# A transformer block on one core: the moving operand of every float32r matmul read as two interleaved halves

## The chip, the cores and the metric

The kernel runs on one core of a Trainium2 chip. A core has a matrix engine (TensorE, called PE in the profile, with its weight loads as PEld), VectorE (DVE), ScalarE (ACT), GpSimd (POOL), and SyncE (SP), which issues the DMAs here. The metric is the device time of one launch in microseconds. Three runs of the kernel before gave 734.32, 734.81 and 735.09 us; their median is 734.81.

## The reference

The input x has 2048 tokens of 448 elements. The program is one pre-norm transformer block: causal attention in a sliding window of 256 tokens with 16 heads of 28 elements, then a GEGLU feed-forward with 1792 hidden columns.

```python
def _A_ref(x, wqkv, wo):          # H = 16, Dh = 28, W = 256
    qkv = ...(x @ wqkv)...
    scores = jnp.einsum("bhqd,bhkd->bhqk", q, k) * (Dh ** -0.5)
    mask = (idx[:, None] - idx[None, :] >= 0) & (idx[:, None] - idx[None, :] < W)
    scores = jnp.where(mask[None, None], scores, -1e9)
    o = jnp.einsum("bhqk,bhkd->bhqd", _softmax(scores, axis=-1), v)
    return (...o...) @ wo

def _B_ref(x, w_gate, w_up, w_down):
    h = _gelu(x @ w_gate) * (x @ w_up)
    return h @ w_down

h = x + _A_ref(_layernorm(x), A_wqkv, A_wo)
h2 = h + _B_ref(_layernorm(h), B_w_gate, B_w_up, B_w_down)
```

Everything is float32.

## The kernel before

**Numbers.** Most products run as float32r matmuls, a float32 format that TensorE takes in one pass. To keep the accuracy of float32, an operand is split into a high part (a copy rounded to float32r, `to_hi`, line 327, on ACT) and a low part (the remainder, `to_lo`, line 330, on DVE or POOL). A product is then a sum of terms: high times high, high times low, low times high. For a contraction over 448 rows, `TERMS` lists 11 matmuls that accumulate into one PSUM bank.

**Attention.** Four groups of four heads by four chunks of 512 tokens make 16 blocks. For each, `project_tile` (line 569) computes queries and keys transposed, with 512 tokens as moving columns (line 580); ACT and DVE take the bank as high and low part (lines 584 and 585), and DMAs carry both through DRAM into the tiles rq and rk. `values` (line 530) computes v with 224 moving columns (line 535) and ACT copies it out (line 538). `scores` (line 621) computes scores of up to 384 keys (line 629), and DVE adds the mask and takes the row maximum (line 633). `maxima` carries the negated maxima into extra rows of rq, so that `probs` (line 693) gives shifted, transposed scores (line 701), from which ACT's exponential writes the tile pp (line 705). `attend` multiplies pp with v in plain float32, four 29-column matmuls side by side (line 735), `drain` divides by the row sums, and `output` (line 770) applies wo with six matmuls of 448 columns (line 779); DVE adds the result to the residual hres (line 782).

**Feed-forward.** The 14 slices of 128 hidden columns are taken in groups of 3, 4, 4 and 3; for each group the kernel goes through the four chunks of 512 tokens, which makes 56 products. The first four (n = 0 to 3) use full 128-row matmuls (line 927) for gate and up. From n = 4 on, a product issues pairs of 64-row matmuls (`pair`, line 899, matmul on line 903): one works in the upper and one in the lower half of the array, on different banks. Phase 0 has 10 pairs of 512 columns and phase 1 has 11, with the halves exchanged; the down product of an earlier hidden slice adds 12 pairs of 448 columns, six between the phases and six after them. Where halves change banks, `seen` (line 909) lets ACT read one word of the bank, so that the next matmul into it waits for the first phase. ACT applies GELU straight from the bank (line 965), DVE multiplies with the other bank (line 967), ACT and DVE split the result (lines 969 and 970). The last down product has 12 full matmuls (line 992), and DVE adds each finished bank to hres (line 998).

**Order.** The instructions are not issued where they stand. Each is registered with `op(engine, cost, latency, key, function, reads, writes, bank)`, and `Lists.run` simulates the six queues with these costs, picks the next instruction of each engine by key among those that can start, and assigns PSUM banks. `mm(n)` is the planner's cost of a matmul of n columns. Engines then run their own queues in order and wait on semaphores. In the feed-forward the order of the matmuls is fixed by a chain of dependences at the end of `feed_forward`.

## Time and profile before

The profiled execution took 734.23 us, of which the span from the first to the last instruction is 732.5 us.

| what | value |
|---|---|
| median of three runs | 734.81 us |
| profiled execution | 734.23 us, span 732.5 us |
| PE busy | 723.8 us, 99% |
| PE weight loads busy | 604.6 us, 83% |
| DVE, ACT, POOL busy | 395.9, 365.8, 160.3 us |
| mean granted TensorE clock | 0.999 |
| HBM read, written | 48.23 MB, 29.36 MB |

The page gives each engine's busy time and share of the span, then the chain of work that ended last, followed back from the last instruction. Rows of groups give line, engine, operation, output and input tiles, shapes and count, then the busy time and the mean ns of one, then the idle time before the group and what ended it. Rows of the timeline give the start, the time from that start to the end of the last of a merged run, and the count. A matmul's recorded time includes its way through the array, so consecutive matmuls overlap in the record, and the distance between starts tells what one costs.

### The profile page before, as it was taken

What the parts mean: (1) busy time and instruction counts of PE and PEld (TensorE: products, weight loads), DVE (VectorE), ACT (ScalarE), POOL (GpSimd) and SP (SyncE); (2) the same over time, 40 slices, a digit from 0 to 9 for tenths busy, and PEclk for the clock granted to TensorE, in tenths of its full rate; (3) what the DMA queues carried; (4) which work ended last, traced back from release to release, by engine and by line L of the source; (5) the groups of instructions that cost most, each with busy time, mean ns of one, the idle gap of its engine ahead of it and who ended that gap; (6) DMA issues with size and microseconds to landing.
All of it is one profiled execution on the core that took longest, in us unless ns stands there. A gap on an engine that the chain in (4) does not pass through costs nothing.

```text
span 732.5 us, 15381 instructions
## 1 busy us (share of the span) xinstructions
PE 723.8 (99%) x5893; PEld 604.6 (83%) x5893; DVE 395.9 (54%) x1057; ACT 365.8 (50%) x930; POOL 160.3 (22%) x253
## 2 busy tenths in 40 slices
PE   8999999999999999999999999999999999999997
PEld 7887888788888787768888888888888888888886
DVE  7977876776677788748554223144223243233223
ACT  7668776667666888876553222243222233222221
POOL 5615343343344547462000000000000000000000
PEclk9999999999999999999999999999999999999999
DMA  8888445755565777514652000012100000001012
GB/s 285 260 280 248 146 148 179 202 178 156 162 201 160 191 229 206 147 36 102 153 174 88 1 2 1 1 43 84 43 1 2 1 1 2 1 1 52 11 42 101
DMA packets 83138, 79.12 MB, mean 108 GB/s; under 512 B 34104, under 2 KB 72952, under 8 KB 83064
## 3 DMA queue, kind: packets, MB, share of 16 engines
q1 hardware_dynamic: 83064, 78.14, 35.3%
q8 instruction: 46, 0.75, 0.4%
q14 instruction: 28, 0.23, 0.1%
HBM read 48.23 MB, written 29.36 MB: 106 GB/s over the span
## 4 chain that ended last, share of the span: by engine, by line
PE 93%; ACT 2%; DVE 2%; DMA 1%; issue 1%; POOL 0%; SPq 0%; DVEq 0%; ACTq 0%; POOLq 0%
PE bank L903 52%; PE bank L580 9%; PE bank L701 6%; PE bank L629 6%; PE bank L735 6%; PE bank L535 5%; PE bank L779 5%; PE bank L927 2%; PE bank L383 1%; ACT pp L705 1%; DVE mt L633 1%; ACT xT L328 0%; DVE hres L782 0%; DMA hres<-in_x_dram 0%; PE bank L660 0%
## 5 line engine op out<-in xcount | busy, mean ns | idle before, releaser
L633 DVE CUSTOM_DVE_ANT_0 mt<-bank,mt 128x384 bf16<-128x384 f32 (+2 forms) x256 | 127.5, 524 | 38.2 <-PE bank L629 36.4
L705 ACT ACTIVATE pp<-bank 128x384 f32<-128x384 f32 (+2 forms) x352 | 121.5, 388 | 52.4 <-PE bank L701 46.5
L967 DVE TENSOR_TENSOR mt<-bank,mt 128x512 f32<-128x512 f32 x54 | 37.1, 688 | 139.5 <-ACT mt L965 139.5
L716 POOL TENSOR_SCALAR_AFFINE_SELECT pp<-pp 128x512 f32<-128x512 f32 x120 | 75.5, 642 | 124.8 <-ACT pp L705 115.0
L580 PE MATMUL bank<-xT,proj 128*128 128x512 f32 x308 | 101.2, 402 | 0.0
L701 PE MATMUL bank<-rq,rk 104*128 104x384 f32 (+2 forms) x352 | 96.8, 305 | 0.9 <-ACT pp L705 0.6
L965 ACT ACTIVATE mt<-bank 128x512 f32<-128x512 f32 x54 | 32.2, 596 | 113.5 <-PE bank L903 113.5
L629 PE MATMUL bank<-rk,rq 84*128 84x384 f32 (+2 forms) x256 | 82.7, 344 | 0.1
L903 PE MATMUL bank<-xT,rec 64*128 64x512 f32 x656 | 82.0, 388 | 0.0
L903 PE MATMUL bank<-xT,rk 64*128 64x512 f32 x656 | 82.0, 388 | 0.0
L701 PEld LDWEIGHTS bank<-rq,rk 104*128 104x128 f32 x352 | 64.7, 189 | 19.3 <-ACT pp L705 4.8
L903 PEld LDWEIGHTS bank<-xT,rec 64*128 64x128 f32 x656 | 63.0, 184 | 12.2
L903 PEld LDWEIGHTS bank<-xT,rk 64*128 64x128 f32 x656 | 63.0, 184 | 12.2
L998 DVE TENSOR_TENSOR hres<-bank,hres 128x448 f32<-128x448 f32 x64 | 35.5, 616 | 66.1 <-PE bank L903 63.9
L328 ACT ACTIVATE proj<-mt 128x512 fp32r<-128x512 f32 x54 | 34.1, 631 | 71.8 <-DVE mt L967 52.5
L903 PE MATMUL bank<-xT,proj 64*128 64x512 f32 x533 | 66.7, 388 | 0.0
L909 ACT ACTIVATE word<-bank 1x1 f32<-1x1 f32 x162 | 25.6, 158 | 79.2 <-PE bank L903 78.6
L580 PEld LDWEIGHTS bank<-xT,proj 128*128 128x128 f32 x308 | 55.9, 190 | 6.0 <-issue 0.8
L535 PE MATMUL bank<-proj,xT 128*128 128x224 f32 x352 | 60.2, 278 | 0.1
L903 PEld LDWEIGHTS bank<-xT,proj 64*128 64x128 f32 x533 | 51.1, 184 | 10.1 <-ACT word L909 0.3
L331 DVE TENSOR_TENSOR proj<-mt,proj 128x512 fp32r<-128x512 f32 x54 | 37.3, 691 | 36.8 <-ACT proj L328 28.5
L535 PEld LDWEIGHTS bank<-proj,xT 128*128 128x128 f32 x352 | 53.0, 191 | 1.8 <-DVE hres L782 0.3
(117 smaller groups left out, 1106.6 us busy)
## 6 DMA issues: line engine op xcount, KB each, us to landing
rk<-k SPq DMA_DIRECT2D x44, 336.0 KB
rq<-q SPq DMA_DIRECT2D x32, 336.0 KB
q<-proj SPq DMA_DIRECT2D x15, 448.0 KB
raw<-in_ffn_dram SPq DMA_DIRECT2D x7, 736.0 KB
v<-in_ffn_dram SPq DMA_DIRECT2D x7, 736.0 KB
k<-proj SPq DMA_DIRECT2D x11, 448.0 KB
hres<-in_x_dram SPq DMA_DIRECT2D x16, 224.0 KB
out_dram<-hres SPq DMA_DIRECT2D x16, 224.0 KB
```

The lines of the kernel that those rows point to most:

```text
L331: (eng or nc.vector).tensor_sub(dst, src, f(hi))
L535: op("pe", mm(224), 0.29, key + a / 16, lambda a=a, h=h, wb=wb, xb=xb: nc.tensor.matmul(bank[b.k][:, 0:224], xT[:, xb, t * 128:(t + 1) * 1 ...
L580: op("pe", mm(512) + 0.002, 0.403, key, lambda a=a, h=h, wb=wb, xb=xb: nc.tensor.matmul(bank[b.k], wqk[i][:, h, wb, :], xT[:, xb, c * 512: ...
L629: nc.tensor.matmul(bank[b.k][:, o:384], rq[u][0:3 * DH, j, i * 128:i * 128 + 128], rk[u][0:3 * DH, j, m0 * 128:(i + 3) * 128], start=True, ...
L633: nc.vector.tensor_tensor_reduce(junk[s % 2][:, o:384], bank[b.k][:, o:384], mask[:, o:384], 1.0, -BIG, OP.add, OP.max, mx[i // 2][:, i % ...
L701: nc.tensor.matmul(bank[b.k][:, 0:n], rk[u][0:104, j, m * 128:m * 128 + 128], rq[u][0:104, j, lo * 128:(hi + 1) * 128], start=True, stop=True)
L705: nc.scalar.activation(pp[:, j, o * 128:o * 128 + n], bank[b.k][:, 0:n], AF.Exp, scale=SCALE)
L716: nc.gpsimd.affine_select(a, a, pattern=[[0, 4], [-cm, 128]], compare_op=op_, fill=0.0, base=0, channel_multiplier=cm)
L735: nc.tensor.matmul(bank[b.k][32 * j:32 * j + DH + 1, lo * 128:(hi + 1) * 128], v[:, 4 * c - 2 + m, g % 2, j, :], pp[:, j, at[m] * 128:(at[ ...
L779: op("pe", mm(D), 0.38, wk, lambda a=a, h=h, oh=oh, wh=wh, i=i, k=k: nc.tensor.matmul(bank[k.k][:, 0:D], ohl[:, h, oh, i * 128:(i + 1) * 1 ...
L903: nc.tensor.matmul(bank[bk.k][:, 0:n], w, m, start=bool(start), stop=bool(stop), tile_position=(64 * x, 0), skip_group_check=True)
L967: op("dve", 0.605, 0.702, key + 2 * NP, lambda: nc.vector.tensor_tensor(blocks(g2), src(1), blocks(g2), op=OP.mult), [*G2, *held[1]], G2, ...
```

## The change

All large float32r products go through a new helper `mul`. It hands TensorE the same stationary operand and the same moving operand, but the moving columns are read in the order 0, n/2, 1, n/2 + 1 and so on. The results still land in PSUM one after the other, so a bank now holds the two halves of its columns interleaved. Every reader of such a bank reads it with a step of two, first half then second half (`unmixed`), and its other operands and its output are written as two halves (`plain`), which are the same addresses in the same order as before. For v the two halves are the two groups of four heads, and the reader takes them apart. The transposes (line 383), the product that carries the maxima (line 660) and `attend` (line 735) stay as they were. The planner's cost of a matmul is changed too.

```diff
 def mm(n):
-    return max(n / 2400 + 0.0155, 0.115)
+    return max(n / 2400 + 0.004, 0.112)
...
+    def mixed(ap):
+        return ap.rearrange("p (h t) -> p t h", h=2)
+
+    def unmixed(ap):
+        return ap.rearrange("p (t h) -> p h t", h=2)
+
+    def plain(ap):
+        return ap.rearrange("p (h t) -> p h t", h=2)
+
+    def mul(o, w, m, **how):
+
+        nc.tensor.matmul(o.rearrange("p (t h) -> p t h", h=2), w, mixed(m), **how)
...
-            op("pe", mm(224), 0.29, key + a / 16, lambda a=a, h=h, wb=wb, xb=xb: nc.tensor.matmul(
+            op("pe", mm(224), 0.29, key + a / 16, lambda a=a, h=h, wb=wb, xb=xb: mul(
...
-            v[:, t, :, :, 0:DH], bank[b.k][:, 0:224].rearrange("p (g h d) -> p g h d", g=2, h=4)), ["ones"], [V(t)], b)
+            v[:, t, :, :, 0:DH], bank[b.k][:, 0:224].rearrange("p (h d g) -> p g h d", g=2, h=4)), ["ones"], [V(t)], b)
...
-        op("act", 0.49, 0.605, key, lambda: to_hi(hl[0], bank[b.k]), (), [tok[0]], b)
-        op("dve", 0.603, 0.698, key, lambda: to_lo(hl[1], bank[b.k], hl[0]), [tok[0]], [tok[1]], b)
+        op("act", 0.49, 0.605, key, lambda: to_hi(plain(hl[0]), unmixed(bank[b.k])), (), [tok[0]], b)
+        op("dve", 0.603, 0.698, key, lambda: to_lo(plain(hl[1]), unmixed(bank[b.k]), plain(hl[0])), [tok[0]], [tok[1]], b)
...
-            nc.tensor.matmul(bank[b.k][:, o:384], rq[u][0:3 * DH, j, i * 128:i * 128 + 128],
+            mul(bank[b.k][:, o:384], rq[u][0:3 * DH, j, i * 128:i * 128 + 128],
...
-            nc.vector.tensor_tensor_reduce(junk[s % 2][:, o:384], bank[b.k][:, o:384], mask[:, o:384],
+            nc.vector.tensor_tensor_reduce(plain(junk[s % 2][:, o:384]), unmixed(bank[b.k][:, o:384]), plain(mask[:, o:384]),
...
-            nc.tensor.matmul(bank[b.k][:, 0:n], rk[u][0:104, j, m * 128:m * 128 + 128],
+            mul(bank[b.k][:, 0:n], rk[u][0:104, j, m * 128:m * 128 + 128],
...
-            nc.scalar.activation(pp[:, j, o * 128:o * 128 + n], bank[b.k][:, 0:n], AF.Exp, scale=SCALE)
+            nc.scalar.activation(plain(pp[:, j, o * 128:o * 128 + n]), unmixed(bank[b.k][:, 0:n]), AF.Exp, scale=SCALE)
...
-                hres[:, t, :], bank[k.k][:, 0:D], hres[:, t, :], op=OP.add), [HR(t)], [HR(t)], k)
+                plain(hres[:, t, :]), unmixed(bank[k.k][:, 0:D]), plain(hres[:, t, :]), op=OP.add), [HR(t)], [HR(t)], k)
...
-                nc.tensor.matmul(bank[bk.k][:, 0:n], w, m, start=bool(start), stop=bool(stop),
+                mul(bank[bk.k][:, 0:n], w, m, start=bool(start), stop=bool(stop),
                                  tile_position=(64 * x, 0), skip_group_check=True)
...
-            return blocks(raw[q] if early else bank[bs[q].k])
+            return plain(raw[q]) if early else unmixed(bank[bs[q].k])
...
-            blocks(g2), src(0), AF.Gelu_apprx_tanh), held[0], G2, bs[0], after=exps)
+            plain(g2), src(0), AF.Gelu_apprx_tanh), held[0], G2, bs[0], after=exps)
...
-            blocks(g2), src(1), blocks(g2), op=OP.mult), [*G2, *held[1]], G2, bs[1], port=early)
+            plain(g2), src(1), plain(g2), op=OP.mult), [*G2, *held[1]], G2, bs[1], port=early)
...
-                    hres[:, t, :], bank[b.k][:, 0:D], hres[:, t, :], op=OP.add), [HR(t)], [HR(t)], down[q])
+                    plain(hres[:, t, :]), unmixed(bank[b.k][:, 0:D]), plain(hres[:, t, :]), op=OP.add), [HR(t)], [HR(t)], down[q])
```

The matmuls of lines 580, 779, 927 and 992 and the copy of line 950 are edited in the same way.

11 lines of the change are left out of this document (6 added, 5 removed).

## The prediction

> **What bounds the kernel now.** I read the page first, parts 1 and 4, to see which engine is busy and whether the chain that ended last runs through it; then the busy times by stage, because a share over the whole span would mix two very different stages; then the chain in order of time.
>
> ```profile
> PE 723.8 (99%) x5893; PEld 604.6 (83%) x5893; DVE 395.9 (54%) x1057; ACT 365.8 (50%) x930; POOL 160.3 (22%) x253
> ...
> PE 93%; ACT 2%; DVE 2%; DMA 1%; issue 1%; POOL 0%; SPq 0%; DVEq 0%; ACTq 0%; POOLq 0%
> ...
> 20.00:341.89 321.89, 319.72 (x2279) 258.76 (x2277) 242.52 (x793) 234.39 (x580) 145.21 (x210) 1.00 0.61 180
> 341.89:725.87 383.98, 383.76 (x3505) 328.26 (x3505) 135.97 (x228) 116.13 (x327) 3.32 (x8) 1.00 0.12 38
> ...
> 400.00:500.00 100.00, 100.00 (x918) 85.69 (x916) 29.67 (x47) 26.88 (x77) 0.00 (x0) 1.00 0.05 16
> ...
> 346.57 379.30 PE bank L903 x3462
> ```
>
> The first two rows say TensorE. Its busy share alone would not prove much, since a matmul's recorded time includes its fill and overlaps with the next one; the chain does, with 93% of the span on PE. The stage rows (PE, weight loads, DVE, ACT, POOL, granted clock, DMA share, GB/s) split the span. From 341.89 to 725.87 us, the feed-forward, DVE works 35% and ACT 30% of the time, and one unbroken chain piece of 379.30 us is PE on line 903. From 20 to 341.89 us, attention, DVE is at 75% and ACT at 73%, so PE is the bound with less room behind it. The clock is full in both. So what matters is the distance from one matmul to the next, which I call a slot.
>
> **What a slot holds.** Line 903 issues two 64-row matmuls together, and they share a slot. Start times come from the timeline:
>
> ```profile
> 449.78 1.30 PE L903 MATMUL bank<-xT,rec 64*128 64x512 f32 x10
> 450.92 1.38 PE L903 MATMUL bank<-rk,proj 64*128 64x448 f32 x12
> 452.13 2.22 PE L903 MATMUL bank<-xT,rec 64*128 64x512 f32 x18
> ...
> 152.27 0.72 PE L735 MATMUL bank<-pp,v 128*29 128x384 f32 x8
> ...
> 152.59 0.72 PE L735 MATMUL bank<-pp,v 128*29 128x256 f32 x12
> ...
> 152.81 0.62 PE L735 MATMUL bank<-pp,v 128*29 128x256 f32 x12
> ```
>
> Five pairs of 512 columns take 450.92 - 449.78 = 1.14 us, 228 ns each; six of 448 take 1.21 us, 202 ns. The 64 columns between them cost 26 ns, so about 2.4 columns per ns, and the rest of each slot, 228 - 512/2.4 = 15 ns, is excess. Over the clean window of 100.00 us there are 459 pairs; the code issues 52 x 21 = 1092 pairs of 512 and 55 x 12 = 660 of 448, whose streams average 203.3 ns. 100,000/459 = 217.9, so the mean excess is 14.6 ns. Line 735, plain fp32 in groups of four, needs 0.32 us from one start to the next at 384 columns and 0.22 at 256: together 0.54 against 2 x 640/2400 = 0.533 at two array cycles per column, so about 3 ns of excess per group (0 to 8 with the rounding). Both kinds write fp32 into PSUM in order; where the operand advances at half the pace, most of the excess is gone.
>
> By the Trainium skill, "TensorE: Matmul & The Clock Gate", section "Back-to-back issue gap", a warm stream costs N/2.4 + 2.5 ns; with 2.5 left, each slot would give 12.1 ns and the feed-forward about 21.2 us. The rows above agree with it for line 735 and not for the float32r slots, which stand 12 ns over it.
>
> **The change part by part.**
>
> (1) The moving operand is read column 0, N/2, 1, N/2+1 and so on; the results land densely in that order. No row shows such a read, so its price is bounded. Best end: the excess falls to nothing, 14.6 ns saved per slot. Worst end: the pace of line 735, two cycles per column, about 203 ns lost per pair. I take 3 ns left, a gain of 11.6 ns, because each of the two halves then advances once in two columns, the pace at which line 735 shows about 3 ns. This is an inference on the mechanism, the weakest step, and the rivals start from it.
>
> Feed-forward: 1752 pairs x 11.6 = 20.3 us, all on the chain piece shown. The order of phases is chained in the code, so nothing else moves.
>
> Attention has these groups (busy us, mean ns, then idle before):
>
> ```profile
> L580 PE MATMUL bank<-xT,proj 128*128 128x512 f32 x308 | 101.2, 402 | 0.0
> L629 PE MATMUL bank<-rk,rq 84*128 84x384 f32 x224 | 75.5, 355 | 0.1
> L779 PE MATMUL bank<-wos,ohl 128*128 128x448 f32 x192 | 49.0, 373 | 0.0
> L701 PE MATMUL bank<-rq,rk 104*128 104x384 f32 x128 | 43.7, 354 | 0.4 <-ACT pp L705 0.3
> L701 PE MATMUL bank<-rq,rk 104*128 104x256 f32 x112 | 32.2, 306 | 0.5 <-ACT pp L705 0.4
> L927 PE MATMUL bank<-xT,proj 128*128 128x512 f32 x66 | 20.6, 404 | 0.8 <-ACT v L950 0.8
> L535 PE MATMUL bank<-proj,xT 128*128 128x224 f32 x352 | 60.2, 278 | 0.1
> ...
> 13.98 5.18 PE L580 MATMUL bank<-xT,proj 128*128 128x512 f32 x22
> 19.00 0.27 PE L535 MATMUL bank<-proj,xT 128*128 128x224 f32 x1
> ...
> 155.78 0.72 PE L535 MATMUL bank<-proj,xT 128*128 128x224 f32 x5
> ```
>
> Line 580 alone takes 5.02/22 = 228 ns per slot, the same 15 ns of excess, so it isn't an effect of pairing. The six wide groups hold 1030 slots; x 11.6 = 11.9 us. Line 535 has a slot of (0.72 - 0.278)/4 = 111 ns against 93 ns of columns. A weight load of 128 columns stands ahead of each, and I take that, not the stream, as its limit: 0 gained, between 0 and 111 - 96 = 15 ns (5 us over 352). Other users of these engines interfere: PE holds 93% of the chain, about 51 us are elsewhere, nearly all of it ahead of the 379.30 us piece, which is up to a sixth of this stage. As PE gets shorter, DVE, ACT and the transfers end last more often. I take two thirds of 11.9, 8.0 us; ends 0 and 11.9.
>
> (2) Weight loads must fit the shorter slot: 448 columns would come to 190 ns.
>
> ```profile
> L903 PEld LDWEIGHTS bank<-rec,proj x360: 182/184/186, 436.2 to 725.3; 64*128 64x128 f32 x180
> ...
> 158.84 0.34 PE L701 MATMUL bank<-rq,rk 104*128 104x384 f32 x1
> 159.01 0.39 PE L580 MATMUL bank<-xT,proj 128*128 128x512 f32 x1
> ...
> L701 PEld LDWEIGHTS bank<-rq,rk x352: 186/189/194, 48.7 to 326.7; 104*128 104x128 f32 x176
> ```
>
> The 384-column slot is already 0.17 us with loads of 189 ns, so a load longer than the slot doesn't hold it up: 0. If it did, 448-column slots would save no more than a few ns less.
>
> (3) The PSUM readers step by two elements. Rows of the dense reads:
>
> ```profile
> L705 ACT ACTIVATE pp<-bank 128x384 f32<-128x384 f32 x128 | 56.9, 491 | 15.6 <-PE bank L701 13.4 <-POOL ohl L331 0.6 <-DMA q<-proj 0.4
> L705 ACT ACTIVATE pp<-bank 128x128 f32<-128x128 f32 x112 | 26.4, 277 | 20.2 <-PE bank L701 19.6
> L633 DVE CUSTOM_DVE_ANT_0 mt<-bank,mt 128x384 bf16<-128x384 f32 x224 | 117.2, 549 | 31.5 <-PE bank L629 29.8
> L633 DVE CUSTOM_DVE_ANT_0 mt<-bank,mt 128x256 bf16<-128x256 f32 x16 | 6.3, 422 | 2.3 <-PE bank L629 2.2
> L633 DVE CUSTOM_DVE_ANT_0 mt<-bank,mt 128x128 bf16<-128x128 f32 x16 | 4.0, 288 | 4.4 <-PE bank L629 4.3
> L331 DVE TENSOR_TENSOR proj<-bank,proj 128x512 fp32r<-128x512 f32 x26 | 17.9, 689 | 5.8 <-ACT proj L328 5.5
> L782 DVE TENSOR_TENSOR hres<-bank,hres 128x448 f32<-128x448 f32 x32 | 19.8, 618 | 13.1 <-PE bank L779 11.6 <-PE bank L701 1.3
> L328 ACT ACTIVATE proj<-mt 128x512 fp32r<-128x512 f32 x54 | 34.1, 631 | 71.8 <-DVE mt L967 52.5 <-PE bank L903 19.2
> L965 ACT ACTIVATE mt<-bank 128x512 f32<-128x512 f32 x54 | 32.2, 596 | 113.5 <-PE bank L903 113.5
> L967 DVE TENSOR_TENSOR mt<-bank,mt 128x512 f32<-128x512 f32 x54 | 37.1, 688 | 139.5 <-ACT mt L965 139.5
> L331 DVE TENSOR_TENSOR proj<-mt,proj 128x512 fp32r<-128x512 f32 x54 | 37.3, 691 | 36.8 <-ACT proj L328 28.5 <-ACT word L909 8.3
> L909 ACT ACTIVATE word<-bank 1x1 f32<-1x1 f32 x162 | 25.6, 158 | 79.2 <-PE bank L903 78.6
> L761 DVE RECIPROCAL rcp<-oblk 128x16 f32<-128x16 f32 x16 | 4.0, 249 | 0.1
> ```
>
> The slopes are (491 - 277)/256 = 0.84 ns per element on ACT and (549 - 288)/256 = 1.02 on DVE. No row steps through PSUM by two. The only element-wise step is line 761's in SBUF, every 32nd element, 249 ns for 16: far off and mostly fixed cost. I take 0, since the engine's own element pace sets the slope and an access per element is all the pattern asks for; upper end, one more element time per element, 0.84 and 1.02. A gain is not excluded by a row but I see no source for one. In the feed-forward even the upper end is covered: lines 965 and 967 would add 512 x 1.86 ns, about 1 us, to a chain of 0.60 + 0.69 + 0.63 + 0.69 = 2.6 us per product, and a product's 33 pairs last 33 x 217.9 ns = 7.2 us. In attention it is not covered (second rival). Line 538 steps by two as well (224 elements, 32 times). The SBUF operands of these readers only split into two dense runs: 0.
>
> (4) The wait at line 909, which lets phase two of a pair cross banks, is covered by six down pairs, 1.21 us now and 1.14 after; behind the last pair stand at worst a copy of 0.63 us already running on ACT and the line's own 0.16 us. It stays covered: 0. The cover shrinks by 0.07 us; if that were missing each time, 162 x 0.07 = 11 us would come back.
>
> (5) The planner's constants (15.5 ns to 4 ns, floor 115 to 112) cost no instruction but reorder attention. That can move a few us either way: 0, ends -3 and +3.
>
> Sum: 20.3 + 8.0 = 28.3 us off the profiled execution's 734.23 (span 732.5), 705.9; that execution lies 0.6 under the median of the runs, 734.81. I predict 706.5.
>
> **The rivals.**
>
> *The interleaved read is slower.* It decides where a slot of 512 columns comes out above today's 228 ns. At line 735's pace the feed-forward alone gains 1752 x 203 = 356 us, total about 1090 with attention untouched; 5% slower streams, about 10 ns a slot, would give some 17 + 10 = 27 us more, 762. Against it: the excess sits on the float32r stream and not on line 735. For it: neighbours come from addresses up to 1 KB apart, which no row shows. The Trainium skill, "Advanced Engine Details and Errata", section "Memory Cachelines", speaks for this rival: a change of 16-byte line at each access is penalised and two hits on a line are needed; in the new order every access changes line. Chance 9%.
>
> *The step of two in PSUM is dear.* At one more element time, DVE in attention gets 92,160 elements of line 633 and, with two more of line 331 in another tile, some 28,700 of lines 331 and 782, x 1.02 = 123 us more, 242.5 + 123 = 366 us of work, past the stage's 321.9. At 95% occupancy the stage lasts 385, so 734.8 + 63 - 20 = 778. It decides slower from DVE work of (321.9 + 20.3) x 0.95 = 325 us on, about 0.68 ns more per element; under that it only eats the gain (715 to 734). Chance of the slower end 6%; of a part of it, leaving 715 to 733, 7%.
>
> *Nothing moves the slot.* If the excess belongs to the PSUM write or to the exchange of weights, every slot stays and only the plan shifts: 732 to 738. The slots of line 735, which write the same fp32 words at half pace, don't exclude it. Chance 6%: 3% within 0.2% and the rest split.
>
> *Attention gives none.* Then 734.8 - 20.3 = 714.5; inside the forecast's upper end.
>
> **How the numbers follow.** Forecast, with all of attention's ends: 694 (14.6 ns on all, 25.6 + 15 us) to 717, chance 72%; the partial case of the readers reaches to 733, 7%. With no more than 2 in 10 left out the range is 694 to 734, which holds both and a third of the case in which nothing moves. About 0.2% is what a measurement of this kernel can tell from no change (the runs shown lie within 0.1%). Faster: 72 + 7 + 2 = 81%; within: 3%; slower: 9 + 6 + 1 = 16%.
>
> **What would show it.** Right: windows of 100 us in the feed-forward hold about 485 pairs (970 matmuls) instead of 459, line 903's chain piece is near 360 us, line 705's and 633's means are within a few ns, line 535's slot stays near 111. Wrong: means of lines 705, 633 and 965 up by more than 100 ns at 384 to 512 columns (second rival), or 918 matmuls or fewer in the same window (first and third). An attention stage above 318 us would mean that another engine took its place.

## The result and the profile after

The changed kernel takes 706.98 us (median of four runs, 706.16 to 711.52) against 734.95 for the kernel before (four runs beside them, 734.32 to 735.50). The ratio is 0.9632, with a 95% interval of 0.9590 to 0.9674. The profiled execution took 706.49 us, its span 704.5; before it was 734.23 and 732.5, so 27.7 us went from the execution and 28.0 from the span. The forecast was 706.5.

In the kernel after, the lines stand 13 or 14 further down, and all matmuls of the helper `mul` carry its line, L338. L646 is line 633 of before, L718 is 705, L922 is 909, L979 is 965, L981 is 967; L341 and L344 are `to_hi` and `to_lo`, L1012 is the sum of line 998.

The page of after, parts 1 and 4 (busy time, share of the span and instructions of each engine; shares of the chain that ended last):

```profile
PE 691.4 (98%) x5893; PEld 603.6 (86%) x5893; DVE 395.3 (56%) x1057; ACT 363.3 (52%) x930; POOL 158.7 (23%) x253
...
PE 91%; DVE 3%; ACT 3%; DMA 1%; issue 1%; POOL 0%; DVEq 0%; ACTq 0%; SPq 0%
```

The same instructions, and the same engine at the bound; DVE and ACT hold a point more of the chain each. PE's busy time fell by 32.4 us, more than the span did, so some idle time came in its place.

The busy times of after in the attention stage and in 100 us of the feed-forward (window, its length, then busy us and instructions of PE, weight loads, DVE, ACT and POOL, then the granted clock, the DMA share and GB/s):

```profile
20.00:334.86 314.86, 309.61 (x2277) 254.61 (x2275) 241.19 (x793) 234.44 (x583) 144.33 (x210) 1.00 0.63 185
400.00:500.00 100.00, 100.00 (x972) 91.77 (x970) 36.12 (x58) 30.19 (x84) 0.00 (x0) 1.00 0.07 24
```

The first of these windows ends where that of the kernel before, 20 to 341.89 us, ends: at the first pair of the feed-forward (2277 matmuls here; the 2279 there take that pair in). The timelines around that place and at the last sums into the residual (start, time to the end of the last of the run, count, idle time before), first in before, then in after:

```profile
341.82 4.53 PE L903 MATMUL bank<-proj 64*128 64x448 f32 x42
346.57 0.87 PE L903 MATMUL bank<-proj 64*128 64x448 f32 x6 [0.22 <-ACT word L909]
347.28 1.09 PE L903 MATMUL bank<-xT,proj 64*128 64x512 f32 x8
727.20 2.21 DVE L998 TENSOR_TENSOR hres<-bank,hres 128x448 f32<-128x448 f32 x4 [2.19 <-PE bank L992]
...
334.86 5.02 PE L338 MATMUL bank<-proj 64*128 64x448 f32 x48
341.22 2.43 PE L338 MATMUL bank<-xT,proj 64*128 64x512 f32 x20 [1.34 <-DVE mt L981]
699.21 2.22 DVE L1012 TENSOR_TENSOR hres<-bank,hres 128x448 f32<-128x448 f32 x4 [2.03 <-PE bank L338]
```

Three things are to be read here. First, 100 us of the feed-forward now hold 972 matmuls, 486 pairs, so a slot takes 100,000/486 = 205.8 ns instead of 217.9. The columns take 203.3 of them, and the excess is 2.5 ns where it was 14.6. Second, the 28.0 us fall into three stretches. The feed-forward's first pair comes 341.82 - 334.86 = 7.0 us sooner; that is attention's part. From there to the first pair of 512 columns, the entry of the feed-forward, after takes longer, 6.4 us instead of 5.5: PE waits 1.34 us for DVE's product (L981), where before it waited 0.22 us. From the first pair of 512 to the last sums it takes 358.0 us instead of 379.9, which is 21.9 us. Behind that nothing changed. Third, in the attention stage PE's idle time grew from 2.2 us (321.89 - 319.72, in the prediction's row) to 314.86 - 309.61 = 5.3 us, at the same work.

The timeline of after at one place in the feed-forward (start, time to the end of the last of the run, count; two matmuls to a slot):

```profile
442.51 1.30 PE L338 MATMUL bank<-rk,proj 64*128 64x448 f32 x12
443.64 2.32 PE L338 MATMUL bank<-xT,rec 64*128 64x512 f32 x20
445.80 0.54 PE L338 MATMUL bank<-rk,proj 64*128 64x448 f32 x4
```

Ten pairs of 512 columns take 445.80 - 443.64 = 2.16 us, 216 ns each (228 before); six of 448 take 1.13 us, 188 ns (202 before). Both sizes lost 12 to 14 ns, which is what the window gives as the mean.

The groups of after that answer to the readers shown before (line, engine, operation, shapes and count, then busy us and mean ns, then idle before):

```profile
L646 DVE CUSTOM_DVE_ANT_0 mt<-bank,mt 128x384 bf16<-128x384 f32 x224 | 117.5, 551 | 33.3 <-PE bank L338 31.3
...
L718 ACT ACTIVATE pp<-bank 128x384 f32<-128x384 f32 x128 | 56.2, 492 | 12.1 <-PE bank L338 11.3
...
L344 DVE TENSOR_TENSOR proj<-mt,proj 128x512 fp32r<-128x512 f32 x54 | 37.4, 692 | 35.4 <-ACT proj L341 28.2 <-ACT word L922 7.0
L981 DVE TENSOR_TENSOR mt<-bank,mt 128x512 f32<-128x512 f32 x54 | 37.2, 689 | 129.7 <-ACT mt L979 129.6
...
L979 ACT ACTIVATE mt<-bank 128x512 f32<-128x512 f32 x54 | 32.2, 597 | 110.0 <-PE bank L338 109.0 <-DVE proj L344 1.0
```

Reading PSUM with a step of two costs 2 ns at most here: 551 ns against 549, 492 against 491, 597 against 596, 689 against 688. The wait on ACT's one-word reads ahead of the split (L344) is 7.0 us, 8.3 before, and it still has PE's work beside it: after's chain is one piece of PE work from 341.22 us on for 357.89 us.

### The profile page after: what moved, and what is told of

Its sections match the earlier page's. It is cut to its first block, busy times and chain, and to the rows that moved or that the text cites. A ratio compares the mean times of both kernels' runs of the same rounds, so it can differ in the third digit from the quotient of the medians.

```text
span 704.5 us, 15350 instructions
## 1 busy us (share of the span) xinstructions
PE 691.4 (98%) x5893; PEld 603.6 (86%) x5893; DVE 395.3 (56%) x1057; ACT 363.3 (52%) x930; POOL 158.7 (23%) x253
## 4 chain that ended last, share of the span: by engine, by line
PE 91%; DVE 3%; ACT 3%; DMA 1%; issue 1%; POOL 0%; DVEq 0%; ACTq 0%; SPq 0%
PE bank L338 85%; PE bank L748 6%; DMA rk<-k 1%; ACT pp L718 1%; DVE proj L344 1%; ACT rq L341 1%; DVE xT L344 1%; PE bank L396 1%; ACT xT L341 1%; PE bank L673 0%; DVE bnst L373 0%; ACT proj L341 0%; DMA hres<-in_x_dram 0%; DVE mt L646 0%; DVE rk L522 0%
## 5 line engine op out<-in xcount | busy, mean ns | idle before, releaser
L338 PE MATMUL bank<-xT,proj 64*128 64x512 f32 (+1 forms) x907 | 175.2, 382 | 2.1 <-DVE mt L981 1.3
L646 DVE CUSTOM_DVE_ANT_0 mt<-bank,mt 128x384 bf16<-128x384 f32 (+2 forms) x256 | 127.9, 526 | 39.4 <-PE bank L338 37.2
L718 ACT ACTIVATE pp<-bank 128x384 f32<-128x384 f32 (+2 forms) x352 | 123.2, 389 | 50.0 <-PE bank L338 46.0
L338 PEld LDWEIGHTS bank<-xT,proj 64*128 64x128 f32 (+1 forms) x907 | 117.9, 188 | 14.6 <-DVE mt L981 1.7
L981 DVE TENSOR_TENSOR mt<-bank,mt 128x512 f32<-128x512 f32 x54 | 37.2, 689 | 129.7 <-ACT mt L979 129.6
L338 PE MATMUL bank<-rq,rk 104*128 104x384 f32 (+2 forms) x352 | 99.2, 301 | 2.0 <-ACT pp L718 1.5
L979 ACT ACTIVATE mt<-bank 128x512 f32<-128x512 f32 x54 | 32.2, 597 | 110.0 <-PE bank L338 109.0
L338 PEld LDWEIGHTS bank<-rq,rk 104*128 104x128 f32 x352 | 65.0, 189 | 19.5 <-ACT pp L718 7.6
L922 ACT ACTIVATE word<-bank 1x1 f32<-1x1 f32 x162 | 25.5, 157 | 107.7 <-PE bank L338 107.4
L338 PE MATMUL bank<-rk,rq 84*128 84x384 f32 (+2 forms) x256 | 78.7, 334 | 2.0 <-DMA rk<-k 1.6
L338 PE MATMUL bank<-xT,rk 64*128 64x512 f32 x656 | 77.7, 376 | 0.0
L338 PE MATMUL bank<-xT,rec 64*128 64x512 f32 x656 | 77.7, 376 | 0.0
L338 PEld LDWEIGHTS bank<-xT,rec 64*128 64x128 f32 x656 | 63.6, 186 | 7.2
L338 PEld LDWEIGHTS bank<-xT,rk 64*128 64x128 f32 x656 | 63.6, 186 | 7.2
L1012 DVE TENSOR_TENSOR hres<-bank,hres 128x448 f32<-128x448 f32 x64 | 35.5, 617 | 60.4 <-ACT mt L979 33.8
L338 PE MATMUL bank<-proj,xT 128*128 128x224 f32 x352 | 58.1, 276 | 0.3 <-DVE xT L344 0.3
L344 DVE TENSOR_TENSOR proj<-mt,proj 128x512 fp32r<-128x512 f32 x54 | 37.4, 692 | 35.4 <-ACT proj L341 28.2
L338 PEld LDWEIGHTS bank<-rk,rq 84*128 84x128 f32 x256 | 46.7, 190 | 8.4 <-issue 3.4
L338 PEld LDWEIGHTS bank<-proj,xT 128*128 128x128 f32 x352 | 51.9, 191 | 1.9 <-DVE xT L344 0.8
L341 ACT ACTIVATE proj<-mt 128x512 fp32r<-128x512 f32 x54 | 34.0, 629 | 28.7 <-DVE mt L981 28.6
L338 PE MATMUL bank<-wos,ohl 128*128 128x448 f32 x192 | 46.4, 365 | 0.1
```

The lines of the kernel that those rows point to most:

```text
L338: nc.tensor.matmul(o.rearrange("p (t h) -> p t h", h=2), w, mixed(m), **how)
L341: nc.scalar.activation(dst, src, AF.Copy)
L344: (eng or nc.vector).tensor_sub(dst, src, f(hi))
L646: nc.vector.tensor_tensor_reduce(plain(junk[s % 2][:, o:384]), unmixed(bank[b.k][:, o:384]), plain(mask[:, o:384]), 1.0, -BIG, OP.add, OP. ...
L718: nc.scalar.activation(plain(pp[:, j, o * 128:o * 128 + n]), unmixed(bank[b.k][:, 0:n]), AF.Exp, scale=SCALE)
L922: op("act", 0.08, 0.17, key, lambda: nc.scalar.activation(word[0:1, 0:1], bank[b.k][0:1, 0:1], AF.Copy), (), (), b)
```

## The experiments

The questions were these. Is it the order of the moving columns that shortens the slot, and which property of the order? Does a step of two in PSUM cost anything for any reader? How do the parts of the change add up? And what keeps attention from giving all that its slots give? The theory at the outset was that of the prediction: each half advances at half the pace. Its rivals were that any spread of the addresses does it, that neighbours from one 16-byte line matter, and that the planner's constants carry part of the gain.

### Streams by themselves

A kernel with no block in it runs 22 matmuls of each order, one after the other, and then copies PSUM out in three ways.

```diff
+    for a in range(R):      # L57: in order
+        nc.tensor.matmul(B(a, 4), W(a), m, **how(a))
+    for a in range(R):      # L59: two halves
+        nc.tensor.matmul(B(a, 6).rearrange("p (t h) -> p t h", h=2), W(a), m.rearrange("p (h t) -> p t h", h=2), **how(a))
+    for a in range(R):      # L61: four quarters
+        nc.tensor.matmul(B(a, 0).rearrange("p (t h) -> p t h", h=4), W(a), m.rearrange("p (h t) -> p t h", h=4), **how(a))
...
+    for a in range(R):      # L65: two halves of each 8 columns
+        nc.tensor.matmul(B(a, 4).rearrange("p (a t h) -> p a t h", h=2, t=4), W(a), m.rearrange("p (a h t) -> p a t h", h=2, t=4), **how(a))
...
+    for k in range(3):      # L94: PSUM read with a step of two
+        nc.scalar.activation(res, bank[k].rearrange("p (t h) -> p h t", h=2), AF.Copy)
```

> This kernel leaves the whole computation out: it holds chains of 22 float32r matmuls of 128x128 by 512 columns, one chain per way of reading the moving operand, and then copies of banks with different steps; its output is not the block's. What counts is the mean distance between starts in each chain. Dense read: 228 ns (the slot of before). Two halves interleaved: 216 ns (the slot of after). Theory A, pace (each of two places in memory is read at half the pace, wherever they are): every alternation of two places comes to about 216, also one within four neighbouring words (order 0, 2, 1, 3), four halves too; a single stream with a step of 2, 4 or 16 words stays at 228. Theory B, neighbourhood (consecutive reads from the same few words collide): 0, 2, 1, 3 stays at 228, alternation of 4, 8 or 16 words away comes to 216 from some distance on, and a single stream with a step of 16 words comes to 216 as well. Theory C, lines are penalised: everything that leaves a line at each read is slower than 228; the result of after speaks against it, but only at distances of 64 words and more. Alternating two words at a time (0, 1, 256, 257): A 216, B 228 or between. Dense bf16: 216; plain fp32: about twice the columns, 430 for one matmul or more. 256 and 128 dense columns: 118 and 60 in the stream, or 111 if the weight load limits the narrow one. Copies of 512 words from PSUM with a step of 2: same as dense within 10 ns on ACT (596) and DVE.

Timeline of this kernel, PE alone (start, time to the end of the 22nd, count); the distance from one start to the next, over 22, is the slot:

```profile
26.55 5.15 PE L57 MATMUL bank<-xin,w 128*128 128x512 f32 x22
31.54 4.91 PE L59 MATMUL bank<-xin,w 128*128 128x512 f32 x22
36.29 6.39 PE L61 MATMUL bank<-xin,w 128*128 128x512 f32 x22
42.51 5.16 PE L63 MATMUL bank<-xin,w 128*128 128x512 f32 x22
47.50 4.91 PE L65 MATMUL bank<-xin,w 128*128 128x512 f32 x22
52.25 4.91 PE L67 MATMUL bank<-xin,w 128*128 128x512 f32 x22
...
61.74 10.09 PE L71 MATMUL bank<-xin,w 128*128 128x512 f32 x22
71.65 9.71 PE L73 MATMUL bank<-xin,w 128*128 128x512 f32 x22
...
101.26 7.52 PE L79 MATMUL bank<-xin,w 128*128 128x512 f32 x22
108.61 7.50 PE L81 MATMUL bank<-xin,w 128*128 128x512 f32 x22
```

| order of the moving columns | line | ns per matmul |
|---|---|---|
| 0, 1, 2, 3 | L57 | 226.7 |
| two halves: 0, 256, 1, 257 | L59 | 215.8 |
| four quarters: 0, 128, 256, 384, 1 | L61 | 282.7 |
| halves of each 4: 0, 2, 1, 3, 4, 6 | L63 | 227.0 |
| halves of each 8: 0, 4, 1, 5, 2, 6 | L65 | 215.8 |
| halves of each 16, of each 32 | L67, L69 | 215.8 |
| one stream with a step of 2 (evens, then odds) | L71 | 450 |
| one stream with a step of 16, of 4, of 2 | L73, L75, L77 | 433, 461, 451 |
| pairs: 0, 1, 256, 257 (L81 writes them in pairs, too) | L79, L81 | 334 |
| bf16, in order | L83 | 215.8 |

With nothing else in the kernel the order alone takes 226.7 to 215.8 ns, and the granted clock was 1.00 from 26.55 to 139.10 us, through all these streams. How far apart the two halves lie makes no difference: 4 columns do as well as 256. So it is not a spread over addresses, and "each half at half the pace" is not enough either: halves of each four columns give nothing (227.0). The orders that go wrong by steps, by quarters or by pairs are the rival that the prediction held at 9%: they cost 283 to 461 ns. None of the three theories put down for this run prices the whole table: A has halves of each four and the quarters at 216 and a step at 228, B has a step of 16 at 216, and C has the two halves above 228.

The copies from PSUM in the same run, by shape (busy us, mean ns, idle before): L92 and L98 read in order, L94 and L100 with a step of two, L96 with a step of 16.

```profile
L92 ACT ACTIVATE res<-bank 128x512 f32<-128x512 f32 x8 | 4.8, 597 | 128.2 <-PE bank L89 128.1
...
L98 DVE COPY res<-bank 128x512 f32<-128x512 f32 x3 | 2.1, 692 | 153.2 <-ACT res L96 153.1
L100 DVE COPY res<-bank 128x512 f32<-128x512 f32 x3 | 2.1, 691 | 0.1
...
L94 ACT ACTIVATE res<-bank 128x512 f32<-128x512 f32 x3 | 1.8, 597 | 0.1
L96 ACT ACTIVATE res<-bank 128x512 f32<-128x512 f32 x3 | 1.8, 597 | 0.1
```

A step of two costs neither reader anything, and a step of 16 costs ACT nothing (DVE's three copies with a step of 16 took 691 ns, too). The Trainium skill, "PSUM — Partial Sum Buffer", section "Specifications (TRN2)", names 8-byte lines and says of patterns that aren't contiguous that they slow matmuls; for the readers of PSUM the runs show no such price. Of writes there is one row: L81 reads the same pairs as L79 and writes them back to the places of the two halves, two results here and two there, and both take 334 ns. A matmul that writes each single result with a step was not tried.

### The same question by lines of four words

The table has one reading that covers nearly all of it. Say that the columns at even and at odd places of the order are taken by two readers in turn, and that each reader gets four aligned words (16 bytes of float32r) at once. In order, the even reader takes columns 0 and 2, then 4 and 6: two of four words used. In two halves it takes 0, 1, 2, 3: all four. By the table four used words are free, two cost 11 ns a matmul, and one doubles the slot. The next kernel chose orders that this reading and its rivals price differently: each column twice, halves read with a step, halves that begin off the four-word boundary, and bf16, where 16 bytes hold eight columns.

```diff
+    for a in range(R):      # L60: each of 256 columns twice
+        nc.tensor.matmul(B(a, 6).rearrange("p (t h) -> p t h", h=2), W(a), xin[:, 0:256, None].to_broadcast([128, 256, 2]), **how(a))
+    for a in range(R):      # L62: halves, each with a step of 2
+        nc.tensor.matmul(B(a, 0).rearrange("p (t h) -> p t h", h=2), W(a), xin[:, 0:1024].rearrange("p (h t w) -> p t h w", h=2, w=2)[:, :, :, 0], **how(a))
...
+    for a in range(R):      # L68: halves of each 8, one word further on
+        nc.tensor.matmul(B(a, 6).rearrange("p (a t h) -> p a t h", h=2, t=4), W(a), xin[:, 1:513].rearrange("p (a h t) -> p a t h", h=2, t=4), **how(a))
...
+    for a in range(R):      # L82: bf16 with a step of 2
+        nc.tensor.matmul(B(a, 4), wb[:, 0:128], xbf[:, 0:1024].rearrange("p (t h) -> p t h", h=2)[:, :, 0], **how(a))
```

> Again chains of 22 matmuls of 512 columns and no block (its output is not the block's). The first chains fit this theory, D: the columns are taken by two readers in turn, one for the even and one for the odd places of the order, and each fetches four float32 words at a time from an address that is a multiple of four; four columns per fetch and reader cost nothing (216 ns), two cost 11 ns per matmul (227, the dense read), one costs twice the time (433 to 461). Rival B: what counts is only that consecutive columns are some words apart. Chains, in order. Dense: D 227, B 227. Each column twice (0, 0, 1, 1, ...): D 216, B 227. Two halves, each with a step of 2 words: D 227, B 216. Two halves, each with a step of 4 words: D 433 to 461, B 216. Blocks of four words alternating (0, 4, 1, 5, ...) from an aligned address: both 216; from an address one word on: D 227 or between, B 216; two words on: D 227, B 216. Two halves from an address two words on: both 216. Dense from one and from two words on: D 227 or a little more, B 227. Two halves 258 words apart: both 216. bf16 dense: 216; with a step of 2, 4, 8 and 16 elements: D, if one fetch brings 16 bytes here too and both readers share the work, 216 or 227, then 227 to 450, then 433 to 461 twice; B gives no forecast.

Timeline of this kernel, PE alone, columns as before:

```profile
26.93 5.15 PE L58 MATMUL bank<-xin,w 128*128 128x512 f32 x22
31.91 4.91 PE L60 MATMUL bank<-xin,w 128*128 128x512 f32 x22
36.66 5.16 PE L62 MATMUL bank<-xin,w 128*128 128x512 f32 x22
41.65 10.13 PE L64 MATMUL bank<-xin,w 128*128 128x512 f32 x22
51.61 4.93 PE L66 MATMUL bank<-xin,w 128*128 128x512 f32 x22
56.37 6.03 PE L68 MATMUL bank<-xin,w 128*128 128x512 f32 x22
62.24 5.16 PE L70 MATMUL bank<-xin,w 128*128 128x512 f32 x22
67.24 4.93 PE L72 MATMUL bank<-xin,w 128*128 128x512 f32 x22
...
91.89 5.13 PE L82 MATMUL bank<-xbf,wb 128*128 128x512 bf16 x22
96.86 10.10 PE L84 MATMUL bank<-xbf,wb 128*128 128x512 bf16 x22
106.78 19.98 PE L86 MATMUL bank<-xbf,wb 128*128 128x512 bf16 x22
126.58 20.37 PE L88 MATMUL bank<-xbf,wb 128*128 128x512 bf16 x22
```

| order | line | words used per fetch | ns per matmul |
|---|---|---|---|
| in order | L58 | 2 | 226.7 |
| each column twice | L60 | 4 | 215.8 |
| halves, each with a step of 2 | L62 | 2 | 227.0 |
| halves, each with a step of 4 | L64 | 1 | 452 |
| halves of each 8 | L66 | 4 | 216.7 |
| the same, one word further on | L68 | 3 and 1 | 266.7 |
| the same, two words further on | L70 | 2 | 227.3 |
| two halves, two words further on; halves 258 apart | L72, L78 | 4 | 216.6 |
| in order, from one word on; from two | L74, L76 | 2 | 236.6, 234.0 |
| bf16 in order; step of 2; of 4 | L80, L82, L84 | 4, 2, 1 columns | 216.3, 225.9, 450.8 |
| bf16, step of 8; of 16 | L86, L88 | 1 column | 900, 918 |

The two-reader reading prices eight of the eleven float32r orders here to within 1 ns or, for a step of 4, within its range. It has the other three only by their order: the two shifted streams in order stand 7 to 10 ns over 226.7, and the fetches of 3 and 1 words, expected at "227 or between", came to 266.7. L60 against L62 decides against the prediction's mechanism: in both each half advances at half the pace, and only the one that uses four words of a fetch is free. It also decides against "far apart" (L60 takes both neighbours from one address). Alignment counts: L66, L68 and L70 are the same order from word 0, 1 and 2.

The last row misses the expected 433 to 461 ns by a factor of two. The granted clock fell to half in the course of L86, which would seem to explain it. The windows of L84, of the first two matmuls of L86, and of L88 show that it does not (columns as above; the granted clock stands third from the end):

```profile
96.90:106.70 9.80, 9.80 (x23) 2.48 (x22) 0.00 (x0) 0.00 (x0) 0.00 (x0) 1.00 0.01 2
106.78:108.50 1.72, 1.72 (x3) 0.23 (x2) 0.00 (x0) 0.00 (x0) 0.00 (x0) 1.00 0.00 0
...
126.60:146.00 19.40, 19.40 (x23) 2.64 (x21) 0.00 (x0) 1.19 (x2) 0.00 (x0) 0.50 0.00 0
```

The first three matmuls of L86 start at 106.78, 107.68 and 108.58 us. So the first two took 900 ns each while the clock was still granted in full (it fell at 108.51), and those at half clock took 900 ns as well. A bf16 stream with a step of 8 is therefore about four times as slow as one in order by itself, and the two-reader reading has no price for that. The step of 16 (918 ns) was measured at half clock alone.

The Trainium skill, "Advanced Engine Details and Errata", section "Memory Cachelines", says that SBUF lines have 16 bytes, that a new line at each access is penalised, and that two hits on a line are needed. Steps and quarters bear that out. Counted column by column it fails here, though: the two halves change lines at every column and are the fastest order (215.8 ns), and pairs hit each line twice in a row and take 334. What these runs suggest is that the lines have to be counted for every second column by itself. Then the order of the kernel before is the one with just two hits, and it still pays 11 ns; the interleaved one has four. By the Trainium skill, "TensorE: Matmul & The Clock Gate", section "Back-to-back issue gap", the isolated gap of a warm matmul is N/2.4 + 2.5 ns, which makes an estimate of about 215.8 ns for 512 columns. The trace agrees with it for bf16 and for interleaved float32r, not for float32r in order (226.7).

Two more rows stay open. Four quarters (283) and pairs (334) make each reader alternate between two lines; with one line kept they would cost the double, with two kept they would be free, and they lie between.

### The parts of the change alone

The feed-forward alone (its matmuls on `mul`, its readers with the step), attention and the planner's constants as before:

```diff
 def mm(n):
-    return max(n / 2400 + 0.004, 0.112)
+    return max(n / 2400 + 0.0155, 0.115)
...
-            mul(bank[b.k][:, o:384], rq[u][0:3 * DH, j, i * 128:i * 128 + 128],
+            nc.tensor.matmul(bank[b.k][:, o:384], rq[u][0:3 * DH, j, i * 128:i * 128 + 128],
...
-            nc.scalar.activation(plain(pp[:, j, o * 128:o * 128 + n]), unmixed(bank[b.k][:, 0:n]), AF.Exp, scale=SCALE)
+            nc.scalar.activation(pp[:, j, o * 128:o * 128 + n], bank[b.k][:, 0:n], AF.Exp, scale=SCALE)
...
```

> Interleaved reads and stepped readers in the feed-forward alone (lines 903, 927 and 992 of before), attention and the planner's constants as before. Theory (slots add up): 1752 pairs times 12.1 ns, 21.2 us, and 100 early matmuls, 1.2: 734.9 - 22 = 713. Rival (the whole 28 us needs both, since the feed-forward starts earlier only if attention ends earlier): the same number here, but then attention's part must come out at 6 to 7 us. If ACT or DVE had become the bound in the feed-forward: above 716.

714.33 us, 0.9721 of before (0.9707 to 0.9736): 20.4 us of the gain. Its window in the feed-forward:

```profile
500.00:600.00 100.00, 100.00 (x970) 90.98 (x967) 31.73 (x51) 28.38 (x82) 0.00 (x0) 1.00 0.03 9
```

Attention alone, with the new constants and the feed-forward in order:

```diff
-                mul(bank[bk.k][:, 0:n], w, m, start=bool(start), stop=bool(stop),
+                nc.tensor.matmul(bank[bk.k][:, 0:n], w, m, start=bool(start), stop=bool(stop),
...
-            return plain(raw[q]) if early else unmixed(bank[bs[q].k])
+            return blocks(raw[q] if early else bank[bs[q].k])
...
```

> Interleaved reads and stepped readers in attention alone, planner's new constants; the feed-forward reads densely. If the parts add up: 734.9 - (28.0 - 20.5) = 727.4, between 726 and 729. If attention's gain exists only together with the other part: 731 or more.

730.71 us, 0.9942 (0.9929 to 0.9955): 4.0 us, less than if the parts added up and just short of the rival's 731, which the interval (729.5 to 731.4) holds. Its window in the feed-forward is that of the kernel before again:

```profile
500.00:600.00 100.00, 100.00 (x916) 85.67 (x916) 30.94 (x50) 25.91 (x75) 0.00 (x0) 1.00 0.05 16
```

The two gains, 20.4 and 4.0, make 24.4 of 28.0. The constants bear on this, as the next two runs show. The change with the old constants:

```diff
 def mm(n):
-    return max(n / 2400 + 0.004, 0.112)
+    return max(n / 2400 + 0.0155, 0.115)
```

> The changed kernel with the planner's old cost of a matmul (15.5 ns over its columns, floor 115), so attention is ordered as in before. If the shorter slots alone make attention's part: 707 to 709, as after. If the new order makes part of it: 710 to 713. If the new order cost something (idle time of PE ahead of its matmuls is larger in after): 703 to 706.

708.81 us, 0.9642 (0.9624 to 0.9660). The interval overlaps that of the whole change, 0.9590 to 0.9674, so the 1.8 us between the medians isn't told from nothing; it is the time expected if the shorter slots alone make attention's part. Against the feed-forward alone, which has the same constants, attention's part here is 714.33 - 708.81 = 5.5 us.

The kernel before with the new constants, no stream changed:

```diff
 def mm(n):
-    return max(n / 2400 + 0.0155, 0.115)
+    return max(n / 2400 + 0.004, 0.112)
```

> The kernel before with the planner's new cost of a matmul and nothing else, so all reads dense. If the order alone is worth nothing: 734 to 736. If an order planned for shorter slots than the chip has costs time: 736 to 741. If it helps by itself: under 733.

737.84 us, 1.0045 (1.0031 to 1.0058): 3.2 us slower. An order planned for slots that the chip does not have costs something, though no instruction is added.

The timelines of the profiled executions, one of each kernel, tell where each gain lies. The stretches are those of the result: up to the feed-forward's first pair, from there to its first pair of 512 columns, and from there to the end of the span (us):

| kernel | constants | up to the first pair | entry | from the first 512 to the end |
|---|---|---|---|---|
| before | old | 341.8 | 5.5 | 385.2 |
| after | new | 334.9 | 6.4 | 363.3 |
| feed-forward alone | old | 341.0 | 5.2 | 365.6 |
| attention alone | new | 337.4 | 6.3 | 385.2 |
| after, old constants | old | 335.4 | 5.3 | 367.0 |
| before, new constants | new | 342.7 | 6.3 | 385.1 |

Up to the first pair the two parts gain 0.8 and 4.4 us of the whole change's 7.0. Behind the first pair of 512 the feed-forward alone gains 19.6 us of 21.9, and attention alone nothing. So the missing 3.6 us lie on both sides of the entry. Behind it they go with the constants: with interleaved reads this stretch takes 365.6 and 367.0 us under the old constants and 363.3 under the new, while with reads in order it takes 385.2 and 385.1. The entry takes about 1 us longer under the new constants, whichever way the columns are read; PE waits there for DVE's product. That the planner's costs reach into the feed-forward, whose matmuls have a fixed order, was not expected; which instructions wait longer there was not taken apart.

### Blocks of two and of four in the kernel

If the reading by four words holds in the block too, halves of each four columns must leave the feed-forward's slot at that of before, and halves of each eight must bring it to that of after. In these two kernels `scores` and `values` kept the halves of the change. The edit for two columns (for four, t is 4):

```diff
     def mixed(ap):
-        return ap.rearrange("p (h t) -> p t h", h=2)
+        return ap.rearrange("p (a h t) -> p a t h", h=2, t=2)

     def unmixed(ap):
-        return ap.rearrange("p (t h) -> p h t", h=2)
+        return ap.rearrange("p (a t h) -> p a h t", h=2, t=2)
...
```

> The changed kernel, but most matmuls read 0, 2, 1, 3, 4, 6, 5, 7 and so on, and their readers step by two within blocks of four; values and scores keep the two halves (their readers can't be written otherwise). Same number of instructions, the same stepped PSUM reads. Theory D (and the chain of the first run that read so): slots stay at 228, 735 to 738, as before_new_constants less up to 3 for scores. If stepping as such made the gain: 707.

> As the last, but in blocks of eight: 0, 4, 1, 5, 2, 6, 3, 7. Theory D: same slots as two halves, 706 to 709. If the halves have to be far apart: 735 to 738.

843.10 us (1.1470, 1.1456 to 1.1485) and 781.08 us (1.0627, 1.0593 to 1.0662): both far over what was expected. The slots of the feed-forward are not the cause. The window of blocks of two:

```profile
500.00:600.00 100.00, 100.00 (x916) 85.58 (x915) 30.82 (x50) 25.60 (x76) 0.00 (x0) 1.00 0.04 14
```

The windows of blocks of four, in the feed-forward and in attention:

```profile
500.00:600.00 100.00, 100.00 (x974) 91.88 (x972) 36.10 (x58) 30.58 (x86) 0.00 (x0) 1.00 0.10 31
20.00:300.00 280.00, 240.24 (x1643) 197.24 (x1643) 173.93 (x591) 159.41 (x389) 94.56 (x140) 0.91 0.52 159
```

And from its waits one that the kernel after doesn't have (who waits for whom, us in total, times, longest):

```profile
PE bank L345 <- DMA rq<-q: 47.0, 13, 5.3
```

916 matmuls in 100 us are the dense slot, 974 the interleaved one: the reading by four words is right in the block as well. The loss is in attention. There PE did 1643 matmuls in the window in which after does 2056, sat idle for 40 us, and had a granted clock of 0.91. The compiled program has 14 waits more than that of after, all on matmuls of `probs`, whose operand rq now has three levels of steps: they wait for the load of the next block's queries, which go into the other half of the same tile. That count is read from the program; the profile shows the 13 long waits. To test it, `probs` alone got the two-level halves back:

```diff
-            mul(bank[b.k][:, 0:n], rk[u][0:104, j, m * 128:m * 128 + 128],
+            halves(bank[b.k][:, 0:n], rk[u][0:104, j, m * 128:m * 128 + 128],
                              rq[u][0:104, j, lo * 128:(hi + 1) * 128], start=True, stop=True)
...
-            nc.scalar.activation(plain(pp[:, j, o * 128:o * 128 + n]), unmixed(bank[b.k][:, 0:n]), AF.Exp, scale=SCALE)
+            nc.scalar.activation(two(pp[:, j, o * 128:o * 128 + n]), bank[b.k][:, 0:n].rearrange("p (t h) -> p h t", h=2), AF.Exp, scale=SCALE)
```

> swap_in_blocks_of_4 was slow in attention, not in its slots. Reading its program against after's, the scores that feed the exponentials (line 701 of before) had 14 waits more, each on the load of the next block's queries, which lie in another half of the same tile; a moving operand with three steps is taken for the whole tile where the waits are derived. Here those matmuls read two halves again, so that every TensorE wait is after's; the projections, output and feed-forward keep the blocks of four words. If the 14 waits made the 74 us: 706 to 709. If something in the blocks themselves (DMA, readers, clock) made them: above 740.

708.20 us, 0.9638 (0.9610 to 0.9666), the same as after within the intervals. The 73 us of the blocks of four were the operand's third level in `probs`: 47.0 us of them stand in the trace as waits, and the rest was not taken apart. They were not the order of the columns, since all other products kept the blocks of four, and blocks of four and halves cost the same by themselves (215.8 ns). In the blocks of two, the trace has the same 13 waits on the load of rq, 42.9 us in all; what else makes up their 108 us over before was not tested.

### What holds attention

In after, PE's idle time ahead of the helper's matmuls between 20 and 330 us is ended by these (us, times):

```profile
  ACT pp L718: 9.4, 25
  issue: 7.3, 19
  DVE mx L646: 3.3, 11
```

L718 is the exponential, L646 the row maximum; both have to free a bank or deliver their result. Two kernels halve the work of one of them.

```diff
-            nc.vector.tensor_tensor_reduce(plain(junk[s % 2][:, o:384]), unmixed(bank[b.k][:, o:384]), plain(mask[:, o:384]),
+            nc.vector.tensor_tensor_reduce(plain(junk[s % 2][:, o:384])[:, 0], unmixed(bank[b.k][:, o:384])[:, 0], plain(mask[:, o:384])[:, 0],
```

> The changed kernel, but DVE's masked row maximum reads only the first half of each bank of scores (its maxima are then not the row's), some 44 us less DVE work in attention at the same order and the same matmuls. Attention gave about 7 us of the 12 that its slots should give. If DVE holds score banks too long for the shorter slots and so keeps the rest: 696 to 703. If the rest is kept by ACT, by loads or by TensorE's own weight loads: 705 to 708.

706.50 us, 0.9622 (0.9606 to 0.9638): no gain that can be told from after's interval, and in the profiled executions the feed-forward's first pair comes 334.86 - 333.89 = 1.0 us sooner. DVE holds attention up by little if at all, although it is the busier of the two.

```diff
-            nc.scalar.activation(plain(pp[:, j, o * 128:o * 128 + n]), unmixed(bank[b.k][:, 0:n]), AF.Exp, scale=SCALE)
+            w = n if B < 3 else n // 2
+            nc.scalar.activation(plain(pp[:, j, o * 128:o * 128 + n])[:, :, 0:w // 2], unmixed(bank[b.k][:, 0:n])[:, :, 0:w // 2], AF.Exp, scale=SCALE)
...
```

> The changed kernel, but in 13 of the 16 blocks ACT's exponential reads and writes only half of its columns, about 31 us less ACT work in attention at the same order and the same matmuls (the rest of the probabilities is left over from earlier blocks, and masked ones become 1e-12 instead of 0, so the output is not the block's). In after the largest idle time of TensorE ahead of its float32r matmuls in attention is on ACT's exponentials, 9.4 us in 25 waits. If ACT, by holding the banks of line 701's scores, keeps the missing 5 us of attention: 698 to 703. If not, as with DVE: 705 to 708.

The edit also sets what the mask's select writes from 0 to 1e-12. 702.53 us, 0.9563 (0.9546 to 0.9579). All its runs (702.23 to 703.95) lie under all those of after. The exponentials hold about 706.98 - 702.53 = 4.4 us. The feed-forward's first pair comes sooner by nearly the same, 334.86 - 330.91 = 3.9 us:

```profile
330.91 5.03 PE L338 MATMUL bank<-proj 64*128 64x448 f32 x48
```

The last kernel leaves all the work in and gives the planner what the runs measured: an excess of 2.5 ns, a floor of 111 ns, and latencies shorter by the 11 to 14 ns that a matmul lost.

```diff
 def mm(n):
-    return max(n / 2400 + 0.004, 0.112)
+    return max(n / 2400 + 0.0025, 0.111)
...
-            op("pe", mm(512) + 0.002, 0.403, key, lambda a=a, h=h, wb=wb, xb=xb: mul(
+            op("pe", mm(512) + 0.002, 0.392, key, lambda a=a, h=h, wb=wb, xb=xb: mul(
...
-        op("pe", mm(n), 0.19 + n / 2400, key, one, q, (), b, tag="prob")
+        op("pe", mm(n), 0.178 + n / 2400, key, one, q, (), b, tag="prob")
...
```

> The changed kernel with the planner told the measured slot (2.5 ns over the columns, floor 111) and matmul latencies 11 to 14 ns shorter, as the record has them. Attempt at a faster version. If a truer plan helps attention as the new constants did against the old ones (about 2 us): 704 to 706. If plans of this accuracy differ only by chance: 704 to 710.

703.24 us, 0.9573 (0.9559 to 0.9587), all four runs between 702.84 and 704.11: the fastest kernel here that leaves nothing out, 3.7 us under after's median and under both forecasts. The intervals of the two ratios, 0.9559 to 0.9587 here and 0.9590 to 0.9674 for after, only just do not meet. It is near what the exponentials hold, but not the same time: in the profiled executions the first pair comes at 333.30 us, 1.6 sooner than in after, and the entry takes 4.9 us instead of 6.4, without the wait for DVE's product. Which operations had to change places for it was not taken apart.

## Why the prediction was right

The time, 706.98 us, is 0.5 from the forecast. That it is so near is in part luck: the feed-forward gave 21.9 us instead of 20.3, attention 7.0 instead of 8.0, and a wait at the entry of the feed-forward, for which the sum had no term, took 0.9 back.

**Step (1), the slot.** 3 ns of excess were to be left; 2.5 are. The feed-forward term, 20.3 us, came out at 21.9 in the change and at 19.6 in the kernel that changes the feed-forward alone (20.4 over the whole kernel). The reason given, that each half then advances at half the pace, was the weakest step, and it was not the reason: halves with a step of two advance at just that pace and stay at 227.0 ns. By that reason halves of each four columns would have had the same price, and they too stay at 227.0. So the right price for the two halves was luck as far as the reason goes. What counts by the runs is how many words of an aligned group of four the even and the odd places of the order use. The rows of line 735 could not have told the two apart; a stream by itself could, in one look.

**Step (1), attention.** 8.0 of 11.9 us were to come, and 7.0 came up to the feed-forward's first pair, of which the entry gave 0.9 back. The direction of the discount was right: PE's idle time in the stage grew by 5.3 - 2.2 = 3.1 us. The mark for another engine in PE's place, a stage above 318 us, was not reached: 334.86 - 20 = 314.9. What holds back a part of the gain is ACT with the exponentials: halving them brings 4.4 us, halving DVE's maxima nothing that can be told from noise. The discount came from a share of the chain; the busy shares (DVE 75%, ACT 73%) would have named the wrong engine. Line 535 was taken at 0: its slot has a median of 111 ns in both traces.

**Step (2), weight loads.** A 448-column slot is now 188 ns and the loads of these pairs take 186. They fit, and 0 was right.

**Step (3), readers of PSUM.** 0 was right to 2 ns in every row, and by itself for a step of two and of 16 on both engines.

**Step (4), the wait at line 909.** It stayed covered: the chain is PE work without a break from the first pair of 512 on.

**Step (5), the constants.** Taken at 0 with ends of 3 us, which is about their size: 3.2 us slower where the slots stay as they were, 1.8 faster here within the noise, and 3.7 us more were left in the order. But the step had them reorder attention alone, and step (1) said that nothing else moves in the feed-forward. By the table of stretches they also cost 1 us at its entry and, with the interleaved reads, save 2.3 to 3.7 us behind it.

**The rivals.** That the read is slower is refuted for this order and true for others near it: with four quarters instead of two halves a stream by itself takes 283 ns a slot. 9% was not too much for it. That a step in PSUM is dear, that nothing moves the slot, and that attention gives none are each refuted by a row above (551 ns, 486 pairs in 100 us, 5.5 us).

**What stays open.** The reading by four words is a model that fits most rows; the hardware behind it was not seen. It leaves open why quarters and pairs cost 283 and 334 ns, and why a bf16 step of 8 costs 900. Open is also what waits in the feed-forward under the old constants, and what in the planner's order is worth 3.7 us.

## What to carry to other kernels

Before tuning around a matmul's slot, run the stream by itself and compare it with columns/2.4 ns: 11 ns of each 512-column slot were lost here to the order in which the moving operand was read, and 8 columns interleaved as two aligned fours (0, 4, 1, 5 and so on) won them back as well as two halves did. Readers of PSUM can undo the order for 2 ns an instruction at most, but an operand with one more level of steps can bring waits on neighbours in the same tile, here worth 73 us, so the number of waits is to be compared whenever an access pattern changes. And when durations change, give the planner the measured ones: an order made for wrong ones cost 3.2 us, one made for the right ones gained 3.7.

## What the runs showed of the hardware that was not expected

- A float32r stream in order is slower than bf16 in order, 226.7 against 215.8 ns for 512 columns, and the interleaved one is as fast as bf16.
- The start of the operand counts: halves of each eight columns take 216.7 ns from word 0, 266.7 from word 1 and 227.3 from word 2.
- A stream with a step is not slower by a share but by a factor: 433 to 461 ns for float32r with a step of 2, 4 or 16, 451 for bf16 with a step of 4, and 900 for bf16 with a step of 8. The bf16 step of 2 costs only 225.9.
- The granted clock fell to 0.50 at 108.51 us, 1.7 us into the bf16 stream with a step of 8, and stayed there to the end of that kernel, although PE had work at every moment up to 146 us. The slot of that stream was 900 ns on both sides of the fall. The bf16 stream with a step of 4 kept 1.00 (96.90 to 106.70 us), and so did 40 us of strided float32r streams (61.74 to 101.26 us of the first stream kernel). What sets the clock back was not tested.
- In the kernel with blocks of four, PE's waits went with a clock of 0.91 in attention, so there they cost more than their own time.
